# Half-height transposes in the visit of y: 64x128 tiles in pairs, with four PSUM banks

## The chip, the cores and the metric

The kernel runs on one core of a Trainium2 chip. The metric is the device time of one execution, in microseconds. The engines are TensorE (PE, with its weight loads shown apart as PEld), VectorE (DVE), ScalarE (ACT), GpSimd (POOL) and SyncE (SP), which here issues nearly all DMAs.

## The reference

Decayed linear attention over 768 tokens, for 4 batches and 8 heads of 64, and then a feed-forward network with softplus on its 3072 tokens:

```python
gamma = 1.0 - 2.0 ** (-5.0 - np.arange(H))
for t in range(S):
    state = gamma * state + k[t] (outer) v[t]      # per batch and head, 64 x 64
    y[t] = (q[t] @ state) / sqrt(64)
x = y as (3072, 512)
h = x @ w_in                                       # 512 -> 2048
g = np.maximum(h, 0.0) + np.log1p(np.exp(-np.abs(h)))
out = g @ w_out                                    # 2048 -> 512
```

q, k, v are float32; w_in and w_out arrive as 64-bit floats and are converted on the chip.

## The kernel before

**Attention.** It works in 24 chunks of 128 tokens (6 per batch), each for all 8 heads. `unit(m, first, G, when)` makes the operations of chunk m; the first chunk comes in two halves, so there are 25 units, and n counts them from 0. A unit loads q, k and v of the chunk (two, two and one DMA on SP), scales q and v on POOL (L419, L415), and then has three visits to TensorE:

1. *Transposes* (tk and tq, L436): eight of 128x128, four of k and four of q, into two PSUM banks; ACT copies each bank to the tile kt (L443, L444).
2. *Scores* (`scores`): 64 matmuls on 64x64 tiles of the array, four side by side: products of k and q, and the chunk's contribution to the state. DVE masks the products (L463) and adds the state (L472).
3. *y* (`outputs`): 64 matmuls on 64x64 tiles, from the state and the masked products. ACT and DVE add the parts together (L541, L547), and ACT and POOL split the sum into a high and a low part in the tile x (L550, L551).

The pairs of banks of the three visits are called tp, sc and yp. From the sixth unit on all of them are taken out of two banks, a0 and a1 (`ATT`).

**The network.** Blocks of 512 tokens, six of them, each in 16 steps of 128 hidden columns (`ffn_step`). A step has twelve matmuls 128x128 by 512 columns into one of two banks hp0 and hp1 (high and low parts: three products for each of four slices of the model's width). DVE, ACT, DVE, ACT and POOL make softplus and split it into gh and gl (L592 to L596); DVE's L594 is the last that reads hp. Then come twelve matmuls into four banks acc0 to acc3, eight with gh and four with gl. All matmuls but the transposes are issued on one helper line, L328. Weights come in tiles of 512 KB and are converted by ACT, DVE and POOL (L352 to L376); a tile's load waits until the tile `2 * FETCH` places before it has been converted.

**The order.** A planner (`Planner.order`) simulates the engines with costs, hand-over times and due times, and writes out a fixed order for each engine; the engines keep to it. `LEAD`, `STAGE` and `PACE` set due times, `SLOW` scales the costs of ACT, DVE and POOL, `KEEP` weighs changes of the array's tiling, `RESERVE` lets an operation hold back from a shared bank for one that is due sooner. `kind` of a TensorE operation is R128 (dense), T128 (transposes) or Q64 (64x64 tiles).

Of the kernel before, what the change touches and what calls it, by code (L numbers as in the profile page):

```python
# [10 lines left out]
F32 = mybir.dt.float32  # L11
# [5 lines left out]
ALU = mybir.AluOpType  # L17
# [9 lines left out]
ST = 4  # L27
QACT = 1
FENCED = 5
SOON = 1  # L30
ORDER = ('c00', 'c01', 'c1', 'h0', 'c2', 'c3', 'h1')
FETCH = 3
SLACK = 2.0**-17

HANDOVER = {
# [60 lines left out]
class Planner:  # L96
# [5 lines left out]
    def add(self, engine, cost, run, after=(), uses=(), at=None):  # L102
        op = Op(engine, cost, run, after, uses, at)
        op.number = len(self.ops)
        op.both, op.earliest, op.kind = False, 0.0, "R128"
        self.ops.append(op)
        return op

    def order(self):
# [16 lines left out]
        def begin(op, since):  # L126
            taken = {}
            for u in op.uses:
                if u.slot is None:
                    if u.ahead is not None and u.ahead.slot is None:  # L130
                        return 1e12
                    n = taken[u.among[0]] = taken.get(u.among[0], 0) + 1
                    since = max(since, sorted(opens(s, op.engine) for s in u.among)[n - 1])
                if u.among[0] in SHARED:
                    for e, end in u.touched.items():
                        if e != op.engine:
                            since = max(since, end + HANDOVER[e][op.engine])
            return since

        while len(out) < len(self.ops):  # L140
            best, fits, wants = None, {}, []
            for e, cands in ready.items():
                fits[e] = []
                for since, op in cands:
                    b = begin(op, since)
                    if b < 1e12:
                        s = max(free[e], b)
                        fits[e].append((s, b, op))
                        wants += [(op.due, s, op, u) for u in op.uses if u.slot is None and u.among[0] in SHARED]
# [67 lines left out]
RESERVE = 200  # L217
SLOW = 1.02
SHARED = ("hp0", "hp1", "acc0", "acc1", "acc2", "acc3", "a0", "a1")
AHEAD = 1.6  # L220
RAMP = 8
COMFORT = {'PE': 0, 'ACT': 0, 'DVE': 0, 'POOL': 0, 'SP': 0}


@with_exitstack
def decay_attention_then_softplus_ffn(ctx: ExitStack, tc: tile.TileContext, q, k, v, w_in, w_out, qtab, vtab, gtab, out):
# [35 lines left out]
    def buf(held):  # L262
        if held.tile is None:
            held.tile = held.make()
        return held.tile
# [40 lines left out]
    def PE(n, run, after, uses=(), at=None, kind="R128"):  # L306
        op = plan.add("PE", n, run, after, uses, at)
        op.kind = kind
        return op

    def ACT(n, run, after, uses=(), at=None):
        return plan.add("ACT", n, run, after, uses, at)
# [65 lines left out]
            wdone[nm, f] = hi, low_  # L378


    xdone, xread, stlast, states, ys = {}, {}, {}, {}, []

    def unit(m, first, G, when):

        n = len(ys)
        b, c = divmod(m, NC)
        E = 2 * G
        hs = slice(4 * first, 4 * (first + G))
# [45 lines left out]
        def transposes(s, held):  # L434
            for e in range(E):
                emit(nc.tensor.transpose(bank(tp[s])[:, e * C:(e + 1) * C], blocks(held)[:, e], ident))  # L436

        old = lambda by: [ys[n - by]] if n >= by else []
        tk = PE(109 * E, lambda: transposes(0, kn), ldk + old(KT), [tp[0], kn], when[0], "T128")
        tq = PE(109 * E, lambda: transposes(1, qn), [dq] + old(KT), [tp[1], qn], when[0], "T128")  # L440
        turned = lambda s: bank(tp[s])[:, :E * C].rearrange("p (e t) -> p e t", e=E)
        ck = [
            ACT(scalar_time(E * C), lambda: emit(nc.scalar.copy(buf(kt)[:, 0, :E], turned(0))), [tk], [tp[0], kt]),  # L443
            ACT(scalar_time(E * C), lambda: emit(nc.scalar.copy(buf(kt)[:, 1, :E], turned(1))), [tq], [tp[1], kt])  # L444
            if QACT else
            DVE(vector_time(E * C), lambda: emit(nc.vector.tensor_copy(buf(kt)[:, 1, :E], turned(1))), [tq], [tp[1], kt]),
        ]
        part = lambda i: slice(i * D, (i + 1) * D)
        parts = 2 if c < NC - 1 else 1

        def scores():
# [25 lines left out]
        for i_ in range(parts):  # L477
            su.append(DVE(vector_time(E * D), lambda i_=i_: update(i_), [s] + su + (stlast[m - 1] if c else []), [sc[i_], st[i_ + 1]] + [x for x in st[i_:i_ + 1] if x]))
        stlast.setdefault(m, []).append(su[-1])

        if n < FENCED:
            def outputs():
# [27 lines left out]
                        for a in range(2):  # L510
                            inner(1 - r, r, g, a)

            y = PE(E * 117 * (2 if c else 1.5) + 240, outputs, ma + su[:1] + [dv] + ck + (stlast[m - 1] if c else []), yp + [vn, ah, kt] + [x for x in st[:2] if x], when[2], "Q64")
            ys.append(y)
            xdeps = [o for j in range(es.start, es.stop) for o in xread.get((i - 2, j), [])]
            xo = lambda t, r: xt[:, t, off // W, es.start + r:es.stop:2, off % W:off % W + C]
            yo = lambda r: bank(yp[r])[:, :G * C].rearrange("p (g t) -> p g t", g=G)
            xhs = [ACT(scalar_time(G * C), lambda r=r: emit(nc.scalar.copy(xo(0, r), yo(r))), [y] + xdeps, [yp[r]]) for r in range(2)]
            xls = [DVE(vector_time(G * C), lambda r=r: emit(nc.vector.tensor_tensor(xo(1, r), yo(r), xo(0, r).bitcast(F32), op=ALU.subtract)), [xhs[r]] + xdeps, [yp[r]]) for r in range(2)]
            done = list(zip(xhs, xls))  # L520
        else:
            xs = hold_xs()

# [13 lines left out]
            y = PE(E * 117 * (2 if c else 1.5), outputs, ma + su[:1] + [dv] + ck + (stlast[m - 1] if c else []), yp + [vn, ah, kt] + [x for x in st[:2] if x], when[2], "Q64")  # L537
            ys.append(y)
            xdeps = [o for j in range(es.start, es.stop) for o in xread.get((i - 2, j), [])]
            xo = lambda t: xt[:, t, off // W, es, off % W:off % W + C]  # L540
            xa = [ACT(scalar_time(E * D), lambda i=i: emit(nc.scalar.copy(buf(xs)[:, :E, part(i)].rearrange("p (g r) t -> p r g t", r=2), second_half(yp[i]).rearrange("p (r g) t -> p r g t", r=2))), [y], [yp[i], xs]) for i in range(2)]  # L541
            tokens = slice(0, C) if c else part(1)

            def add(r):
                st_ = bank(yp[r])[:, :G * C].rearrange("p (g t) -> p g t", g=G)[:, :, tokens]
                part_ = buf(xs)[:, r:E:2, tokens]
                emit(nc.vector.tensor_tensor(part_, st_, part_, op=ALU.add))  # L547

            xb = [DVE(vector_time(E * D // (1 if c else 2)), lambda r=r: add(r), xa, [yp[r], xs]) for r in range(2)]
            xh = ACT(scalar_time(E * C, False), lambda: emit(nc.scalar.copy(xo(0), buf(xs)[:, :E])), xb + xdeps, [xs])  # L550
            xl = POOL(2.53 * E * C, lambda: emit(nc.gpsimd.tensor_tensor(xo(1), buf(xs)[:, :E], xo(0).bitcast(F32), op=ALU.subtract)), [xh] + xdeps, [xs])  # L551
            done = [(xh, xl)] * 2
        for j in range(es.start, es.stop):
            xdone[m, j] = list(done[j % 2])
# [202 lines left out]
```

## Time and profile before

| what | value |
|---|---|
| times of three runs | 631.61, 633.56, 636.33 us |
| median | 633.56 us |
| the profiled execution's own time | 632.99 us |
| its span, first to last instruction | 631.2 us |
| PE busy | 616.8 us (98%) |
| DVE, ACT, POOL busy | 240.3, 223.6, 239.0 us |
| granted TensorE clock | 1.000 |
| DMA moved | 42.79 MB, mean 68 GB/s |

The page gives busy times, the chain of work that ended last (followed back from the last instruction, at each step to what released it), groups of instructions by line and shape, and DMA issues. The timeline's rows have start and length in microseconds, the engine, the line, the operation, what it writes and reads, and how many instructions are merged in the row; a bracket holds the idle time before it and who ended it. Matmuls are pipelined: a record of 0.39 us does not keep the array for 0.39 us. The price of a matmul is the distance to the next one's start.

### The profile page before, as it was taken

How to read it: one execution, taken by the hardware profiler on the slowest of the kernel's cores; microseconds unless marked ns; L12 is line 12 of the kernel's file. 1: busy time of each engine (PE TensorE's matmuls, PEld its weight loads, DVE VectorE, ACT ScalarE, POOL GpSimd, SP SyncE). 2: the span in 40 equal slices, each digit the busy share in tenths (PEclk: the TensorE clock that was granted, in tenths of full speed). 3: DMA queues.
4: the chain of work that ended last, by engine and by line, in shares of the span. 5: the costliest groups of instructions: out<-in, count | busy, mean ns of one | idle time of the engine just before them, and what ended most of it. 6: DMA issues, size and time to landing. Idle time of an engine off the chain costs nothing.

```text
span 631.2 us, 12857 instructions
## 1 busy us (share of the span) xinstructions
PE 616.8 (98%) x5464; PEld 505.8 (80%) x5464; DVE 240.3 (38%) x439; ACT 223.6 (35%) x405; POOL 239.0 (38%) x206
## 2 busy tenths in 40 slices
PE   5889999999999999999999999999999999999997
PEld 4778888778888888888888888888888888888886
DVE  3687789343333223323333223233332322322232
ACT  3577877333223223222233222322332223322221
POOL 3577777553333324233333242333323223212221
PEclk9999999999999999999999999999999999999999
DMA  7997661341211203102113021020320000100001
GB/s 190 276 297 243 199 208 61 69 128 25 51 27 26 51 9 110 34 18 51 24 28 107 18 46 34 18 51 22 97 52 0 2 1 1 67 1 2 0 1 66
DMA packets 90441, 42.79 MB, mean 68 GB/s; under 512 B 77072, under 2 KB 85264, under 8 KB 90384
## 3 DMA queue, kind: packets, MB, share of 16 engines
q1 hardware_dynamic: 89936, 41.95, 24.1%
q8 instruction: 43, 0.70, 0.4%
q14 instruction: 14, 0.11, 0.1%
q10 hardware_dynamic: 448, 0.01, 0.0%
HBM read 35.66 MB, written 6.29 MB: 66 GB/s over the span
## 4 chain that ended last, share of the span: by engine, by line
PE 97%; DMA 1%; ACT 1%; DVE 1%; issue 1%; SPq 0%; POOL 0%; DVEq 0%; ACTq 0%; POOLq 0%
PE acc L328 43%; PE hp L328 43%; PE a L328 7%; PE a L436 3%; DMA qn<-in_q_dram 1%; PE acc L436 0%; DVE ah L463 0%; ACT win L375 0%; DVE a L367 0%; DVE a L362 0%; DVE st L472 0%; POOL qn L419 0%; ACT wout L375 0%; ACT wout L444 0%; ACT w L631 0%
## 5 line engine op out<-in xcount | busy, mean ns | idle before, releaser
L328 PE MATMUL hp<-x,win 128*128 128x512 f32 (+1 forms) x1176 | 289.2, 390 | 0.0
L328 PEld LDWEIGHTS hp<-x,win 128*128 128x128 f32 x1176 | 215.3, 189 | 43.2
L596 POOL TENSOR_TENSOR gl<-sp,gh 128x512 fp32r<-128x512 f32 x90 | 115.9, 1288 | 320.8 <-ACT gh L595 218.9
L328 PE MATMUL acc<-wout,gh 128*128 128x512 f32 x736 | 190.3, 394 | 0.0
L328 PEld LDWEIGHTS acc<-wout,gh 128*128 128x128 f32 x736 | 136.3, 188 | 29.7
L592 DVE TENSOR_SCALAR sp<-hp 128x512 uint32<-128x512 uint32 x92 | 63.5, 690 | 239.2 <-PE hp L328 188.1
L593 ACT ACTIVATE sp<-sp 128x512 f32<-128x512 f32 x92 | 58.1, 632 | 228.2 <-DVE sp L592 228.1
L328 PE MATMUL acc<-wout,gl 128*128 128x512 f32 x368 | 103.0, 390 | 0.0
L594 DVE SCALAR_TENSOR_TENSOR sp<-hp,sp 128x512 f32<-128x512 f32 x92 | 63.5, 690 | 55.6 <-ACT sp L593 55.5
L328 PEld LDWEIGHTS acc<-wout,gl 128*128 128x128 f32 x368 | 69.0, 188 | 14.7 <-POOL gl L596 0.2
L595 ACT CAST gh<-sp 128x512 fp32r<-128x512 f32 x90 | 55.9, 621 | 43.8 <-DVE sp L594 43.0
L443 ACT COPY kt<-a 128x512 f32<-128x512 f32 (+1 forms) x22 | 12.7, 576 | 63.5 <-PE a L436 63.4
L463 DVE TENSOR_TENSOR ah<-a,mask 128x256 uint32<-128x256 uint32 x42 | 15.9, 419 | 36.2 <-PE a L328 36.2
L551 POOL TENSOR_TENSOR x<-xs,x 128x512 fp32r<-128x512 f32 x20 | 25.8, 1289 | 8.9 <-ACT x L550 8.9
L419 POOL TENSOR_TENSOR qn<-qn,tabs 128x512 f32<-128x512 f32 (+1 forms) x23 | 23.8, 1033 | 8.8 <-DMA qn<-in_q_dram 8.6
L415 POOL TENSOR_TENSOR vn<-vn,tabs 128x512 f32<-128x512 f32 (+1 forms) x24 | 24.2, 1008 | 5.7 <-DMA vn<-in_v_dram 5.7
L376 POOL TENSOR_TENSOR wout<-w,wout 128x512 fp32r<-128x512 f32 x16 | 20.7, 1294 | 8.6 <-ACT wout L375 8.6
L376 POOL TENSOR_TENSOR win<-w,win 128x512 fp32r<-128x512 f32 x16 | 20.7, 1297 | 8.0 <-ACT win L375 5.2
L352 ACT ACTIVATE raw<-raw 128x512 f32<-128x512 f32 x32 | 21.2, 677 | 2.4 <-DMA raw<-in_moe_w_in_dram 2.3
L367 DVE SCALAR_TENSOR_TENSOR a<-raw,a 128x512 uint32<-128x512 uint32 x28 | 19.1, 690 | 1.4 <-ACT a L356 1.0
L547 DVE TENSOR_TENSOR xs<-a,xs 128x256 f32<-128x256 f32 (+1 forms) x40 | 14.3, 395 | 12.6 <-ACT xs L541 12.6
L372 DVE SCALAR_TENSOR_TENSOR w<-raw,a 128x512 uint32<-128x512 uint32 x28 | 18.6, 679 | 0.6
(106 smaller groups left out, 377.4 us busy)
## 6 DMA issues: line engine op xcount, KB each, us to landing
raw<-in_moe_w_in_dram SPq DMA_DIRECT2D x16, 512.0 KB, 6.8
raw<-in_moe_w_out_dram SPq DMA_DIRECT2D x16, 512.0 KB, 5.9
qn<-in_q_dram SPq DMA_DIRECT2D x44, 128.0 KB, 2.6
kn<-in_k_dram SPq DMA_DIRECT2D x44, 128.0 KB, 2.8
vn<-in_v_dram SPq DMA_DIRECT2D x22, 256.0 KB, 3.0
out_dram<-w SPq DMA_DIRECT2D x22, 256.0 KB, 2.2
out_dram<-win SPq DMA_DIRECT2D x2, 256.0 KB, 2.1
qn<-in_q_dram SPq DMA_DIRECT2D x4, 64.0 KB, 2.3
```

What stands on the lines that cost most here:

```text
L328: mm = lambda o, l, r, start, stop: emit(nc.tensor.matmul(o, lhsT=l, rhs=r, start=start, stop=stop))
L352: a = ACT(685, lambda word=word: emit(nc.scalar.activation(word(1).bitcast(F32), word(1).bitcast(F32), AF.Copy, scale=2.0**-112)), [ld], [ ...
L367: lambda word=word, wp=wp: emit(nc.vector.scalar_tensor_tensor(bits(wp), word(1), 0x80000000, bits(wp), op0=ALU.bitwise_and, op1=ALU.bitwi ...
L376: low_ = POOL(1300, lambda nm=nm, w=w: emit(nc.gpsimd.tensor_tensor(hl(nm, f)[:, 1], buf(w), hl(nm, f)[:, 0].bitcast(F32), op=ALU.subtract ...
L415: emit(engine.tensor_tensor(heads(held), heads(held), by, op=ALU.mult))
L419: emit(engine.tensor_tensor(all_, all_, by, op=ALU.mult))
L551: xl = POOL(2.53 * E * C, lambda: emit(nc.gpsimd.tensor_tensor(xo(1), buf(xs)[:, :E], xo(0).bitcast(F32), op=ALU.subtract)), [xh] + xdeps, ...
L592: a = DVE(vector_time(T), lambda: emit(nc.vector.tensor_scalar(U(spv()), U(bank(hp)), 0x80000000, None, op0=ALU.bitwise_or)), [lasts[-1]] ...
L593: b = ACT(640, lambda: emit(nc.scalar.activation(spv(), spv(), AF.Softplus)), [a], [sp])
L594: c = DVE(vector_time(T), lambda: emit(nc.vector.scalar_tensor_tensor(spv(), bank(hp), 0.0, spv(), op0=ALU.max, op1=ALU.add)), [b], [hp, sp])
L595: e = ACT(scalar_time(T, False), lambda: emit(nc.scalar.copy(buf(gh), spv())), [c], [sp, gh])
L596: g = POOL(1300, lambda: emit(nc.gpsimd.tensor_tensor(buf(gl), spv(), buf(gh).bitcast(F32), op=ALU.subtract)), [e], [sp, gh, gl])
```

## The change

From the 13th unit on (`MERGED = 12`) the transposes of a unit are no visit of their own. They are sixteen transposes of 64 rows by 128 columns, two for each of the eight blocks, one on the upper and one on the lower half of the rows. Those of the lower half of the tokens go to one bank, those of the upper half to the other, for k and q together; the copies to kt write the halves of the tokens accordingly. They are issued in one operation of the planner together with the y of the unit before (`outputs_and_turn`), whose planning is held back in the list `pending` until the next unit comes. This operation needs four banks, and banks of the attention are now taken out of a0, a1, hp0 and hp1 (`WIDE`). It is "patient": another operation that wants one of its banks holds back when the patient one could start within `HOLD`, 1000 ns. Numbers of the planner change with it (`FETCH`, `KEEP`, `LEAD`, `PACE`, `SLOW`, `COMFORT`).

```diff
+MERGED = 12
+HOLD = 1000
-FETCH = 3
+FETCH = 2
...
                     b = begin(op, since)
+                    if op.patient:
+                        wants += [(op.due, max(free[e], since), op, u) for u in op.uses if u.slot is None and u.among[0] in SHARED]
...
-                        rivals = sum(d < op.due and t < s + RESERVE and o is not op and set(v.among) <= set(u.among) for d, t, o, v in wants)
+                        rivals = sum(d < op.due and t < s + (HOLD if o.patient else RESERVE) and o is not op and not set(v.among).isdisjoint(u.among) for d, t, o, v in wants)
...
-KEEP = 2
+KEEP = 0.5
-LEAD = 2700
+LEAD = -4000
-PACE = 500
+PACE = 0
-SLOW = 1.02
+SLOW = 1.0
+WIDE = ["a0", "a1", "hp0", "hp1"]
-COMFORT = {'PE': 0, 'ACT': 0, 'DVE': 0, 'POOL': 0, 'SP': 0}
+COMFORT = {'PE': 0, 'ACT': 100, 'DVE': 100, 'POOL': 100, 'SP': 0}
...
-        banks = [[hold_bank(ATT[0]) for _ in range(2)] for _ in range(3)]
-        tp, sc, yp = banks
+        merged = n >= MERGED
+        tp = [hold_bank(WIDE if merged else ATT[0]) for _ in range(2)]
+        sc = [hold_bank(WIDE if n >= MERGED else ATT[0]) for _ in range(2)]
+        yp = [hold_bank(WIDE if n + 1 >= MERGED else ATT[0]) for _ in range(2)]
...
+        if merged:
+            def turn():
+                for t, held in enumerate((kn, qn)):
+                    for e in range(E):
+                        for i in range(2):
+                            emit(nc.tensor.transpose(bank(tp[i])[:, (t * E + e) * D:(t * E + e + 1) * D], blocks(held)[side[i], e], ident[side[i], part(i)]))
+
+            tdeps, tuses = ldk + [dq] + old(KT), [*tp, kn, qn]
+            if pending:
+                outputs_, cost_, deps_, uses_, _, finish_ = pending.pop()[1:]
+
+                def outputs_and_turn():
+                    outputs_()
+                    turn()
+
+                tk = tq = PE(cost_ + 58 * 2 * E, outputs_and_turn, deps_ + tdeps, uses_ + tuses, when[0], "Q64")
+                tk.patient = True
+                finish_(tk)
+            else:
+                tk = tq = PE(58 * 2 * E, turn, tdeps, tuses, when[0], "Q64")
+            turned = lambda i: bank(tp[i])[:, :2 * E * D].rearrange("p (s e t) -> p s e t", s=2, e=E)
+            into = lambda i: buf(kt)[:, :, :E, part(i)]
+        else:
...
         ck = [
-            ACT(scalar_time(E * C), lambda: emit(nc.scalar.copy(buf(kt)[:, 0, :E], turned(0))), [tk], [tp[0], kt]),
-            ACT(scalar_time(E * C), lambda: emit(nc.scalar.copy(buf(kt)[:, 1, :E], turned(1))), [tq], [tp[1], kt])
+            ACT(scalar_time(E * C), lambda: emit(nc.scalar.copy(into(0), turned(0))), [tk], [tp[0], kt]),
+            ACT(scalar_time(E * C), lambda: emit(nc.scalar.copy(into(1), turned(1))), [tq], [tp[1], kt])
...
+        deps = ma + su[:1] + [dv] + ck + (stlast[m - 1] if c else [])
+        uses = yp + [vn, ah, kt] + [x for x in st[:2] if x]
+        pending.append((m, outputs, cost, deps, uses, when[2], finish))
+        if n + 1 < MERGED:
+            flush()
+
+    def flush():
+        if pending:
+            m, outputs, cost, deps, uses, due, finish = pending.pop()
+            finish(PE(cost, outputs, deps, uses, due, "Q64"))
...
     def ffn_step(s, h, i, f, when):
+        if pending and pending[0][0] < NT * (i + 1):
+            flush()
```

More of the change, by code (lines that the diff above doesn't have):

```diff
@@ L104, in add @@
         op.number = len(self.ops)
-        op.both, op.earliest, op.kind = False, 0.0, "R128"
+        op.both, op.earliest, op.kind, op.patient = False, 0.0, "R128", False
         self.ops.append(op)
@@ L148, in order @@
                         fits[e].append((s, b, op))
-                        wants += [(op.due, s, op, u) for u in op.uses if u.slot is None and u.among[0] in SHARED]
+                        if not op.patient:
+                            wants += [(op.due, s, op, u) for u in op.uses if u.slot is None and u.among[0] in SHARED]
             def waits(s, op):
@@ L378, in convert_weights @@
             wdone[nm, f] = hi, low_
-    xdone, xread, stlast, states, ys = {}, {}, {}, {}, []
+    xdone, xread, stlast, states, ys, pending = {}, {}, {}, {}, [], []
     def unit(m, first, G, when):
-        n = len(ys)
+        n = len(ys) + len(pending)
         b, c = divmod(m, NC)
@@ L432, in unit @@
         xt = X[i % 2]
-        def transposes(s, held):
-            for e in range(E):
-                emit(nc.tensor.transpose(bank(tp[s])[:, e * C:(e + 1) * C], blocks(held)[:, e], ident))
         old = lambda by: [ys[n - by]] if n >= by else []
-        tk = PE(109 * E, lambda: transposes(0, kn), ldk + old(KT), [tp[0], kn], when[0], "T128")
-        tq = PE(109 * E, lambda: transposes(1, qn), [dq] + old(KT), [tp[1], qn], when[0], "T128")
-        turned = lambda s: bank(tp[s])[:, :E * C].rearrange("p (e t) -> p e t", e=E)
+        part = lambda i: slice(i * D, (i + 1) * D)
@@ new lines, in unit, with transposes @@
+        if merged:
[18 more added lines that the diff above has]
+        else:
+            def transposes(s, held):
+                for e in range(E):
+                    emit(nc.tensor.transpose(bank(tp[s])[:, e * C:(e + 1) * C], blocks(held)[:, e], ident))
+            tk = PE(109 * E, lambda: transposes(0, kn), ldk + old(KT), [tp[0], kn], when[0], "T128")
+            tq = PE(109 * E, lambda: transposes(1, qn), [dq] + old(KT), [tp[1], qn], when[0], "T128")
+            turned = lambda s: bank(tp[s])[:, :E * C].rearrange("p (e t) -> p e t", e=E)
+            into = lambda s: buf(kt)[:, s, :E]
@@ L442, in unit @@
         ck = [
-            ACT(scalar_time(E * C), lambda: emit(nc.scalar.copy(buf(kt)[:, 0, :E], turned(0))), [tk], [tp[0], kt]),
-            ACT(scalar_time(E * C), lambda: emit(nc.scalar.copy(buf(kt)[:, 1, :E], turned(1))), [tq], [tp[1], kt])
+            ACT(scalar_time(E * C), lambda: emit(nc.scalar.copy(into(0), turned(0))), [tk], [tp[0], kt]),
+            ACT(scalar_time(E * C), lambda: emit(nc.scalar.copy(into(1), turned(1))), [tq], [tp[1], kt])
             if QACT else
-            DVE(vector_time(E * C), lambda: emit(nc.vector.tensor_copy(buf(kt)[:, 1, :E], turned(1))), [tq], [tp[1], kt]),
+            DVE(vector_time(E * C), lambda: emit(nc.vector.tensor_copy(into(1), turned(1))), [tq], [tp[1], kt]),
@@ L447, in unit @@
         ]
-        part = lambda i: slice(i * D, (i + 1) * D)
         parts = 2 if c < NC - 1 else 1
@@ L479, in unit, with record @@
         stlast.setdefault(m, []).append(su[-1])
+        def record(done):
+            for j in range(es.start, es.stop):
+                xdone[m, j] = list(done[j % 2])
         if n < FENCED:
@@ L511, in outputs, with finish @@
                             inner(1 - r, r, g, a)
[L513 to L520, printed above, removed]
+            cost = E * 117 * (2 if c else 1.5) + 240
+            def finish(y):
+                ys.append(y)
+                xdeps = [o for j in range(es.start, es.stop) for o in xread.get((i - 2, j), [])]
+                xo = lambda t, r: xt[:, t, off // W, es.start + r:es.stop:2, off % W:off % W + C]
+                yo = lambda r: bank(yp[r])[:, :G * C].rearrange("p (g t) -> p g t", g=G)
+                xhs = [ACT(scalar_time(G * C), lambda r=r: emit(nc.scalar.copy(xo(0, r), yo(r))), [y] + xdeps, [yp[r]]) for r in range(2)]
+                xls = [DVE(vector_time(G * C), lambda r=r: emit(nc.vector.tensor_tensor(xo(1, r), yo(r), xo(0, r).bitcast(F32), op=ALU.subtract)), [xhs[r]] + xdeps, [yp[r]]) for r in range(2)]
+                record(list(zip(xhs, xls)))
         else:
@@ L535, in outputs @@
                                 mm(second_half(yp[i])[side[a], r * G + g], heads(vn)[side[i], 4 * g + 2 * r + a], buf(ah)[side[i], r, a * G + g], True, True)
[L537 to L554, printed above, removed]
+            cost = E * 117 * (2 if c else 1.5)
@@ new lines, in finish, with add @@
+            def finish(y):
+                ys.append(y)
+                xdeps = [o for j in range(es.start, es.stop) for o in xread.get((i - 2, j), [])]
+                xo = lambda t: xt[:, t, off // W, es, off % W:off % W + C]
+                xa = [ACT(scalar_time(E * D), lambda i=i: emit(nc.scalar.copy(buf(xs)[:, :E, part(i)].rearrange("p (g r) t -> p r g t", r=2), second_half(yp[i]).rearrange("p (r g) t -> p r g t", r=2))), [y], [yp[i], xs]) for i in range(2)]
+                tokens = slice(0, C) if c else part(1)
+                def add(r):
+                    st_ = bank(yp[r])[:, :G * C].rearrange("p (g t) -> p g t", g=G)[:, :, tokens]
+                    part_ = buf(xs)[:, r:E:2, tokens]
+                    emit(nc.vector.tensor_tensor(part_, st_, part_, op=ALU.add))
+                xb = [DVE(vector_time(E * D // (1 if c else 2)), lambda r=r: add(r), xa, [yp[r], xs]) for r in range(2)]
+                xh = ACT(scalar_time(E * C, False), lambda: emit(nc.scalar.copy(xo(0), buf(xs)[:, :E])), xb + xdeps, [xs])
+                xl = POOL(2.53 * E * C, lambda: emit(nc.gpsimd.tensor_tensor(xo(1), buf(xs)[:, :E], xo(0).bitcast(F32), op=ALU.subtract)), [xh] + xdeps, [xs])
+                record([(xh, xl)] * 2)
```

## The prediction

> **What bounds the kernel now.** I read the page's busy times and its chain first, then the sums by stretch, then TensorE's waits, then the timeline of one chunk.
>
> ```profile
> span 631.2 us, 12857 instructions
> PE 616.8 (98%) x5464; PEld 505.8 (80%) x5464; DVE 240.3 (38%) x439; ACT 223.6 (35%) x405; POOL 239.0 (38%) x206
> PE 97%; DMA 1%; ACT 1%; DVE 1%; issue 1%; SPq 0%; POOL 0%; DVEq 0%; ACTq 0%; POOLq 0%
> ```
> ```profile
> 0.00:47.00 47.00, 36.35 (x614) 31.02 (x615) 28.19 (x66) 24.78 (x50) 24.32 (x31) 1.00 0.94 254
> 47.00:142.00 95.00, 94.98 (x987) 77.15 (x986) 65.07 (x115) 60.44 (x110) 64.31 (x53) 1.00 0.50 152
> 142.00:521.00 379.00, 379.00 (x3399) 309.94 (x3397) 116.83 (x213) 110.01 (x201) 123.28 (x102) 1.00 0.15 38
> 521.00:631.20 110.20, 106.50 (x476) 87.64 (x468) 30.20 (x45) 28.39 (x47) 27.08 (x21) 1.00 0.05 20
> ```
> ```profile
> PE a L436 <- DVE qn L419: 4.3, 1, 4.3
> PE a L328 <- DVE st L472: 1.5, 1, 1.5
> ```
>
> The columns of the second fence are the stretch, its length, then busy time of PE, weight loads, DVE, ACT and POOL, the granted clock, the DMA share and GB/s. TensorE owns 97% of the chain. From 47 us on it never stands still: 94.98 of 95 us, then 379.00 of 379. The 10.65 us that it idles lie in the first 47 us, where DMA is at 0.94; the largest TensorE wait is the very first, for q. So behind 47 us a change can only win by giving TensorE less to do, and can lose wherever TensorE has to wait. A busy record says little of the price of one instruction, because the records overlap; prices must come from starts. Here is one chunk, with the other engines' rows that matter later.
>
> ```profile
> 298.08 4.24 PE L328 MATMUL hp<-x,win 128*128 128x512 f32 x18
> 302.16 1.98 PE L328 MATMUL acc<-wout,gh 128*128 128x512 f32 x8
> ...
> 306.24 2.00 PE L328 MATMUL acc<-wout,gh 128*128 128x512 f32 x8
> 308.08 1.07 PE L328 MATMUL acc<-wout,gl 128*128 128x512 f32 x4
> 308.99 0.85 PE L328 MATMUL hp<-x,win 128*128 128x512 f32 x3
> 309.68 0.60 PE L436 MATMUL a<-ident,kn 128*128 128x128 f32 x4
> 309.94 0.69 DVE L592 TENSOR_SCALAR sp<-hp 128x512 uint32<-128x512 uint32 x1 [4.63 <-PE hp L328]
> 310.11 0.60 PE L436 MATMUL a<-ident,qn 128*128 128x128 f32 x4
> 310.31 0.59 ACT L443 COPY kt<-a 128x512 f32<-128x512 f32 x1 [4.29 <-PE a L436]
> 310.46 2.30 PE L328 MATMUL hp<-x,win 128*128 128x512 f32 x9
> 310.79 0.64 ACT L593 ACTIVATE sp<-sp 128x512 f32<-128x512 f32 x1
> 311.46 0.69 DVE L594 SCALAR_TENSOR_TENSOR sp<-hp,sp 128x512 f32<-128x512 f32 x1 [0.82 <-ACT sp L593]
> 312.69 0.69 PE L328 MATMUL a<-kt 64*64 64x64 f32 x32
> 313.21 0.65 PE L328 MATMUL a<-vn,kn 64*64 64x64 f32 x32
> 313.79 2.11 PE L328 MATMUL acc<-wout,gh 128*128 128x512 f32 x8
> 315.74 1.07 PE L328 MATMUL acc<-wout,gl 128*128 128x512 f32 x4
> 316.64 0.84 PE L328 MATMUL hp<-x,win 128*128 128x512 f32 x3
> 317.41 0.69 PE L328 MATMUL a<-kt,st 64*64 64x64 f32 x32
> 317.93 0.65 PE L328 MATMUL a<-ah,vn 64*64 64x64 f32 x32
> 318.51 2.34 PE L328 MATMUL hp<-x,win 128*128 128x512 f32 x9
> 318.85 0.63 ACT L541 COPY xs<-a 128x256 f32<-128x256 f32 x2
> 319.59 0.74 DVE L547 TENSOR_TENSOR xs<-a,xs 128x256 f32<-128x256 f32 x2
> 320.68 1.98 PE L328 MATMUL acc<-wout,gh 128*128 128x512 f32 x8
> ```
> ```profile
> L328 PE MATMUL a<-ah,vn 64*64 64x64 f32 x480 | 9.7, 218 | 0.0
> L436 PE MATMUL a<-ident,qn 128*128 128x128 f32 x60 | 9.0, 272 | 0.0
> ```
>
> The visits of a chunk are the transposes (309.68), the scores (312.69) and y (317.41). A dense matmul costs (302.16 − 298.08)/18 = 0.227 us. Whatever a dense run takes beyond that is the price of going in or out of a visit.
>
> **The change part by part.**
>
> *The transposes go.* Their eight starts last 310.46 − 309.68 = 0.78 us. The nine dense matmuls behind them take 2.23 us against 9 × 0.227 = 2.04, so 0.19 too much; 0.09 of it belongs to entering the scores, since the three dense ones ahead of y also take 0.77 instead of 0.68. Leaving the transposes costs 0.10. Removed: 0.88 us per chunk. One transpose costs (0.60 − 0.272)/3 = 0.109 us.
>
> *Sixteen half tiles come.* Each has 64 rows, 128 columns and 64 moving columns, and they stand in pairs, one on either half of the rows. No row of before has this form. The ends: a pair runs at the pace of a set of four 64x64 matmuls, at most (0.65 − 0.218)/7 = 0.06 us, so 8 × 0.06 = 0.48; or a pair costs what a transpose of 128 columns costs, 8 × 0.109 = 0.87; or the two of a pair don't run beside each other, 16 × 0.109 = 1.74. I take 0.06. The reason is in the lengths of the records:
>
> ```profile
> L328 PE MATMUL hp<-x,win 128*128 128x512 f32 x10 | 2.5, 392 | 0.0
> L328 PE MATMUL hp<-x,win 128*128 128x256 f32 x17 | 2.2, 283 | 0.0
> ```
>
> A transpose with 128 moving columns (272 ns) is as long as a dense matmul with 256 (283 ns) and far from the one with 512. A 64x64 one is 54 ns shorter. So both kinds behave as if the moving side set the pace, at some 0.43 ns (109/256) for each of two steps per column, and the moving side is what this change halves. The ends of records are modelled, so this is a leaning and no proof.
>
> The Trainium skill speaks against it: "TensorE: Matmul & The Clock Gate", section "LDWEIGHTS (loading the stationary operand)", says that a load's time follows the stationary columns alone, whatever the rows, at 107 ns for 128. The trace fits that as well (109 ns per transpose, 60 per set with 64 columns), since in every form of before the two sides are equally wide. By that page a pair would cost as much as a whole transpose and the first term of the sum below would be nothing.
>
> *The change of tile inside the visit.* Between y's 64x64 tiles and the 64x128 tiles the array's division changes. Ends: nothing, and the 0.09 + 0.13 = 0.22 us that going in and out of a y visit costs (0.13 is 318.51 to 320.68, 2.17, less 2.04). Half the division, the rows, stays; I take 0.11. The skill's "TensorEngine Tiling (Array Packing)", section "Key Properties", says that every change of mode drains the engine; by it I would take the upper end. Leaving the visit costs what leaving y costs already.
>
> *Sum on TensorE:* 0.88 − 0.48 − 0.11 = 0.29 us for each fused visit. Unit 12's transposes ride on unit 11's y, and so on up to unit 24: 13 visits, 13 × 0.29 = 3.8 us.
>
> *Four banks for a visit.* It needs both y banks and both transpose banks, out of a0, a1, hp0, hp1: all four at once. Before, y needed two and a half-filled hp stayed beside it (316.64 and 318.51). Now TensorE's queue, which is in order, holds the acc and hp matmuls behind a visit that waits for DVE's last read of hp (L594), for DVE's reads of the scores (L463, L472), for POOL's scaled q of the next chunk (L419) and for its k. From TensorE's turning away (309.68) to the end of that L594 (311.46 + 0.69) are 2.47 us. The twelve acc matmuls of the step before are 12 × 0.227 = 2.72, so they cover it with 0.25 to spare, if they all stand there. After the visit the banks come free through two copies of 0.59, two L541 (0.63) and two L547 (0.74): at most 2.55 us one after another, again under 2.72. POOL waits for ACT's gh in this order as before. I take nothing; the upper end is under the rivals. An end below nothing is excluded behind 47 us, since no wait is there to win.
>
> *Moved work.* Copies, masks, y's parts and loads stay the same in number; the two copies write runs of 64, as L541's do at their usual pace. ACT, DVE and POOL are busy under a third of 142 to 521 us, which hides them. Due times of units come 6.7 us earlier (LEAD), those of steps no longer drift (PACE); loads of q, k and v move up on SP past output stores, with DMA at 0.15 there. POOL's scaling moves up past gl; it takes 123 of 379 us. If that cover were gone, a visit would wait for one such operation, about 1 us.
>
> *The start.* FETCH 2 lets four weight tiles be on their way in place of six, and the other planner numbers (KEEP, SLOW, COMFORT, HOLD) may reorder it.
>
> ```profile
> raw<-in_moe_w_in_dram SPq DMA_DIRECT2D x16, 512.0 KB, 6.8
> L367 DVE SCALAR_TENSOR_TENSOR a<-raw,a 128x512 uint32<-128x512 uint32 x28 | 19.1, 690 | 1.4 <-ACT a L356 1.0
> ```
>
> A tile takes 6.8 us to land and five operations of about 0.69, some 10.3 us; four at a time make two tiles in 5.2 us. A step wants two tiles in 24 × 0.227 us plus a quarter of a chunk's visits (a quarter of 3.5), 6.3 us. So the loads stay hidden with 1.1 us a step to spare; without that cover, DVE being busy 65 of 95 us there, each of the 14 later steps could lose a few tenths, 4 us in all. On the other side at most the 10.65 idle us of the start can be won. I take nothing.
>
> The profiled execution took 632.99 us with its span of 631.2; its time lies 0.57 below the median of the runs, 633.56. 632.99 − 3.8 = **629.2 us**.
>
> **The rivals.**
>
> *The pair is held by its 128 columns.* 0.88 − 0.87 − 0.11 = −0.10, times 13: 634.3 us. For it: the equal widths above cannot exclude it. Against it: the record lengths. This is the skill's rule on the load, above.
>
> *Four banks make TensorE wait* (the one that ends slower). Place: ahead of each fused visit. If only the eight gh matmuls are there as cover (1.82 us), 2.47 − 1.82 = 0.65 us is open: 13 × 0.65 = 8.5, less 3.8, gives 637.7 us. With only four gl matmuls it is 1.56 us a visit and 649. It decides from 0.29 us a visit on. For it: hp is never free in the rows above, one half-filled group always lies across a visit. Against it: the planner orders with nearly these durations, and its order of before leaves TensorE no wait behind 47 us.
>
> *The start gets shorter as well*, by a third of its idle time, 3.5 us: 625.7 us. For it: fewer weight tiles ahead of q, k, v at a DMA share of 0.94. Against it: TensorE's first weights, which bound the first dense run, are no earlier.
>
> *The tiles don't run two at a time* (the change does not do what it says): at 0.109 each, 0.88 − 1.74 − 0.11 = −0.97, 645.6 us; at 0.06 each 635.6. Against it: four 64x64 tiles do run together in before.
>
> **How the numbers follow.** Forecast 0.49, column-bound pair 0.22, bank waits 0.14, shorter start 0.10, no pairs 0.05. The range reaches from 625.0 (just past the shorter start) to 637.7 (the first bank-wait case); outside lie the longer bank waits, unpaired tiles at 0.109 and a start shortened further. A measurement of this kernel tells about 1%, 6.3 us, from no change. Faster by over that, below 627.2: the shorter start (0.10), plus the part of the forecast without a price for the change of tile (627.8) and with any gain at the start, 0.12: 0.22. Slower by over it, above 639.9: longer bank waits 0.06, no pairs 0.03, late weights 0.02: 0.11. Within: 0.67.
>
> **What would show it.** Starts of a fused visit's pairs 0.06 apart (right) or 0.11 (rival); the time from y's last start to the first transpose for the change of tile; a chunk from visit to visit in about 25.0 us in place of 25.3; TensorE waits for hp's L594 for the banks; idle TensorE time up to 47 us for the start. The prediction is wrong if pairs cost 0.11 or any wait of TensorE's behind 47 us sums to over 4 us.

## The result and the profile after

The changed kernel takes 629.62 us (median of 6 runs, 628.59 to 631.87) against 633.74 us (6 runs, 631.61 to 636.33) for the kernel before beside it: a ratio of 0.9932 with the interval 0.9906 to 0.9957. The forecast was 629.2. The profiled execution took 629.27 us. First the page of the changed kernel (its span, its busy times, its chain by engine), then its sums by stretch, with the columns of the prediction's second fence:

```profile
span 627.6 us, 13098 instructions
PE 612.6 (98%) x5568; PEld 501.7 (80%) x5568; DVE 242.7 (39%) x439; ACT 225.3 (36%) x405; POOL 239.3 (38%) x206
PE 93%; DMA 2%; issue 1%; POOL 1%; SPq 1%; DVE 1%; ACT 0%; POOLq 0%; DVEq 0%
```
```profile
0.00:47.00 47.00, 37.51 (x685) 31.77 (x686) 29.82 (x71) 25.32 (x50) 26.97 (x33) 1.00 0.92 244
47.00:142.00 95.00, 93.89 (x922) 76.11 (x921) 64.37 (x114) 61.87 (x113) 64.76 (x53) 1.00 0.52 155
142.00:521.00 379.00, 378.36 (x3513) 308.95 (x3512) 119.49 (x214) 112.09 (x202) 122.99 (x102) 1.00 0.15 38
521.00:627.60 106.60, 102.81 (x454) 84.83 (x452) 28.97 (x42) 26.06 (x42) 24.62 (x20) 0.99 0.06 20
```

TensorE is still the bound. There are 104 more matmul records (13 chunks, eight more transposes each), and yet less busy time. What is new is idle time behind 47 us, where before TensorE hardly ever stood still: 1.11 us in the second row, ahead of the fused visits (0.70 for POOL's gl at 59.35, and 0.41 at 93.68 for which the trace names no releaser), and 0.64 us in the third.

One fused visit in the timeline of the changed kernel; L334 is the helper that was L328, L449 the half transposes:

```profile
276.00 0.69 PE L334 MATMUL a<-kt,st 64*64 64x64 f32 x32
276.51 0.65 PE L334 MATMUL a<-ah,vn 64*64 64x64 f32 x32
277.09 0.46 PE L449 MATMUL hp<-ident,kn 64*128 64x64 f32 x8
277.38 0.42 PE L449 MATMUL hp<-ident,qn 64*128 64x64 f32 x8
277.73 1.20 PE L334 MATMUL acc<-wout,gh 128*128 128x512 f32 x4
...
301.05 0.69 PE L334 MATMUL a<-kt,st 64*64 64x64 f32 x32
```
```profile
L449 PE MATMUL hp<-ident,kn 64*128 64x64 f32 x104 | 6.7, 236 | 0.6 <-DVE sp L645 0.4
L449 PE MATMUL hp<-ident,qn 64*128 64x64 f32 x104 | 5.5, 223 | 0.0
```

From the first transpose to the first dense matmul are 277.73 − 277.09 = 0.64 us. The row of q has eight transposes in four pairs and is 0.42 long with one record of 0.223, so its pairs start (0.42 − 0.223)/3 = 0.066 us apart; in the unmerged starts it is 0.0626. Eight pairs make 0.50, and 0.14 is left for the change of tile. A chunk, from one y to the next, takes 301.05 − 276.00 = 25.05 us; before, it was 309.68 − 284.36 = 25.32.

**How the gain divides.** A simple measure: the time from the start of the 11th unit's y to the last dense matmul, less 0.2269 us for each dense matmul started in between. What is left is what the attention's visits and the waits cost. Before (two rows), then after:

```profile
165.68 0.69 PE L328 MATMUL a<-kt,st 64*64 64x64 f32 x32
...
627.12 0.39 PE L328 MATMUL acc<-wout,gl 128*128 128x512 f32 x1
```
```profile
158.79 0.69 PE L334 MATMUL a<-kt,st 64*64 64x64 f32 x32
...
623.42 0.39 PE L334 MATMUL acc<-wout,gl 128*128 128x512 f32 x1
```

Between them stand 1812 dense matmuls before and 1836 after (24 of them moved behind that y). Before: 627.12 − 165.68 − 1812 × 0.2269 = 50.30 us. After: 623.42 − 158.79 − 1836 × 0.2269 = 48.05 us. So 2.25 us are won there, not 3.8. The two executions are 3.72 us apart; the other 1.4 us lie ahead of that point (158.79 + 24 × 0.2269 = 164.24 against 165.68).

**Where the visits lose.** Three of the 13 fused visits wait, at 251.40, 352.31 and 452.79, some 100 us or one block of the network apart. The first one, with the other engines' rows:

```profile
249.54 1.07 PE L334 MATMUL acc<-wout,gl 128*128 128x512 f32 x4
...
250.54 0.46 PE L334 MATMUL a<-kt,st 64*64 64x64 f32 x16
...
250.82 0.65 PE L334 MATMUL a<-ah,vn 64*64 64x64 f32 x32
251.20 0.69 DVE L645 SCALAR_TENSOR_TENSOR sp<-hp,sp 128x512 f32<-128x512 f32 x1 [0.70 <-ACT sp L644]
...
251.40 0.27 PE L449 MATMUL hp<-ident,kn 64*128 64x64 f32 x1
...
252.04 0.43 PE L449 MATMUL hp<-ident,kn 64*128 64x64 f32 x7 [0.37 <-DVE sp L645]
252.28 0.44 PE L449 MATMUL hp<-ident,qn 64*128 64x64 f32 x8
...
252.66 0.73 PE L334 MATMUL acc<-wout,gh 128*128 128x512 f32 x2
```

The first transpose goes to the one hp bank, which is free; the second goes to the other, whose last reader L645 (L594 before) ends at 251.89. TensorE turned away from that bank at 249.54, so the chain of softplus took 2.35 us to that end (the prediction has 2.47), and the next transpose starts 2.50 us after the turning away. In that time TensorE had only four matmuls with gl and a y shortened to 48 matmuls (the first chunk of a batch has no state): 251.40 − 249.54 = 1.86 us. The visit is 1.26 us in place of 0.64. At the other two y is whole and the visits last 1.02. The three cost 0.61 + 0.38 + 0.38 = 1.37 us. With 13 × 0.27 = 3.5 for the chunks, 3.5 − 1.4 = 2.1 stands against the 2.25 measured. In the ten other visits hp was read out long before.

### The profile page after: what moved, and what is told of

Same layout as the page of the kernel before. It is cut to its first block, busy times and chain, and to the rows that moved or that the text cites. A ratio compares the mean times of both kernels' runs of the same rounds, so it can differ in the third digit from the quotient of the medians.

```text
span 627.6 us, 13098 instructions
## 1 busy us (share of the span) xinstructions
PE 612.6 (98%) x5568; PEld 501.7 (80%) x5568; DVE 242.7 (39%) x439; ACT 225.3 (36%) x405; POOL 239.3 (38%) x206
## 4 chain that ended last, share of the span: by engine, by line
PE 93%; DMA 2%; issue 1%; POOL 1%; SPq 1%; DVE 1%; ACT 0%; POOLq 0%; DVEq 0%
PE hp L334 43%; PE acc L334 42%; PE a L334 5%; DMA qn<-in_q_dram 2%; PE hp L449 1%; PE a L469 1%; POOL win L382 0%; SPq L412 0%; POOL qn L425 0%; DVE sp L643 0%; DVE sp L645 0%; SPq L353 0%; ACT sp L644 0%; POOL gl L647 0%; POOL vn L421 0%
## 5 line engine op out<-in xcount | busy, mean ns | idle before, releaser
L334 PE MATMUL hp<-x,win 128*128 128x512 f32 (+1 forms) x1176 | 296.1, 388 | 0.0
L334 PEld LDWEIGHTS hp<-x,win 128*128 128x128 f32 x1176 | 215.5, 188 | 44.0
L334 PE MATMUL acc<-wout,gh 128*128 128x512 f32 x736 | 197.9, 393 | 0.0
L334 PEld LDWEIGHTS acc<-wout,gh 128*128 128x128 f32 x736 | 136.3, 188 | 29.3 <-ACT gh L646 0.2
L644 ACT ACTIVATE sp<-sp 128x512 f32<-128x512 f32 x92 | 58.1, 632 | 247.8 <-DVE sp L643 247.7
L334 PE MATMUL acc<-wout,gl 128*128 128x512 f32 x368 | 103.1, 391 | 0.7 <-POOL gl L647 0.7
L645 DVE SCALAR_TENSOR_TENSOR sp<-hp,sp 128x512 f32<-128x512 f32 x92 | 63.5, 691 | 53.5 <-ACT sp L644 53.1
L334 PEld LDWEIGHTS acc<-wout,gl 128*128 128x128 f32 x368 | 68.9, 188 | 15.6 <-POOL gl L647 1.1
L590 ACT CAST x<-xs 128x512 fp32r<-128x512 f32 x20 | 12.4, 619 | 15.0 <-DVE xs L587 15.0
L334 PEld LDWEIGHTS a<-kt,st 64*64 64x64 f32 x616 | 11.4, 135 | 7.6 <-issue 6.9
```

The costliest lines, as they stand in the source:

```text
L334: mm = lambda o, l, r, start, stop: emit(nc.tensor.matmul(o, lhsT=l, rhs=r, start=start, stop=stop))
L644: b = ACT(640, lambda: emit(nc.scalar.activation(spv(), spv(), AF.Softplus)), [a], [sp])
L645: c = DVE(vector_time(T), lambda: emit(nc.vector.scalar_tensor_tensor(spv(), bank(hp), 0.0, spv(), op0=ALU.max, op1=ALU.add)), [b], [hp, sp])
```

## The experiments

The kernels with other transposes, with plain matmuls, with the half tiles apart and with `HOLD = 0` were timed in a single run each, which can't tell 2 us from nothing on this kernel; they are read from their timelines. The first three and the half tiles apart had one run of the kernel before beside them, of 631.52 us.

**Whole transposes in the fused visit.**

```diff
-                        for i in range(2):
-                            emit(nc.tensor.transpose(bank(tp[i])[...], blocks(held)[side[i], e], ident[side[i], part(i)]))
+                        emit(nc.tensor.transpose(bank(tp[t])[:, e * C:(e + 1) * C], blocks(held)[:, e], ident))
```

> The fused visits keep their place and order, but the transposes in them are eight of 128x128 again, k into one bank and q into the other. Theory (the gain comes from pairs at 0.062 us): first transpose to first dense matmul 8 x 0.109 + 0.145 for the change of tile = 1.02 us in place of 0.645; a chunk 25.4 us in place of 25.05; 13 x 0.37 = 4.9 us more, 634 us. Rival (the gain comes from having one visit less and from the new order): 0.65 to 0.7 us, a chunk near 25.05, 629 to 630 us.

634.39 us. The fused visit in its timeline:

```profile
229.31 0.65 PE L448 MATMUL hp<-ident,kn 128*128 128x128 f32 x4
229.80 0.60 PE L448 MATMUL hp<-ident,qn 128*128 128x128 f32 x4
230.16 1.17 PE L334 MATMUL acc<-wout,gh 128*128 128x512 f32 x4
```

230.16 − 229.31 = 0.85 us, 0.2 more than the half tiles; a chunk is 25.24 us, and the measure above gives 50.57, that is 2.5 us more than after. Of these, 2.1 are ten visits at 0.21 (the three visits that wait for hp last as long as after, 1.25 and 1.02 us), and 0.5 is one wait for DVE's copy out of an acc bank (L683). So the half tiles are worth having, at about half the expected price a visit: among dense matmuls the same eight transposes took 0.78 us, so the change of tile cost the whole ones 0.07, where 0.145 on top of 8 × 0.109 had been expected.

**The same sixteen transposes, all of the upper half's after all of the lower's.**

```diff
-                for t, held in enumerate((kn, qn)):
-                    for e in range(E):
-                        for i in range(2):
+                for i in range(2):
+                    for t, held in enumerate((kn, qn)):
+                        for e in range(E):
```

> The same sixteen 64x128 transposes, but first the eight of the lower rows and then the eight of the upper rows, so that neighbours use the same half of the array. Theory (a pair is two tiles side by side, each held by its 64 moving columns): 16 x 0.062 + 0.145 = 1.14 us in place of 0.645, 13 x 0.5 = 6.4 us more, 635.7 us. Rival A (a tile is held by its 128 loaded columns and only the other half of the rows hid that): 16 x 0.109 + 0.145 = 1.89 us, 16 us more, 645.5 us. Rival B (half a tile has half the price, neighbours do not matter): 0.645 us, 629.3 us.

634.26 us. In its timeline:

```profile
228.90 0.46 PE L449 MATMUL hp<-ident,kn 64*128 64x64 f32 x4
229.19 0.22 PE L449 MATMUL hp<-ident,qn 64*128 64x64 f32 x1
229.20 0.27 PE L449 MATMUL hp<-ident,kn 64*128 64x64 f32 x1
...
229.50 0.41 PE L449 MATMUL hp<-ident,qn 64*128 64x64 f32 x4
229.84 1.20 PE L334 MATMUL acc<-wout,gh 128*128 128x512 f32 x4
```

The visit takes 229.84 − 228.90 = 0.94 us in place of 0.64. As long as only lower tiles run, single ones start 0.0626 us apart, exactly as pairs do in the changed kernel: two at a time cost what one costs. It isn't the whole 0.50 more, because k's upper tiles (from 229.20) start while q's lower ones are still being started. That tiles run in pairs is shown.

**Sixteen plain matmuls with half the moving columns, in the place of the transposes.**

```diff
-emit(nc.tensor.transpose(bank(tp[i])[...], blocks(held)[side[i], e], ident[side[i], part(i)]))
+mm(bank(tp[i])[...], blocks(held)[:, e], ident[:, part(i)], True, True)
```

> The same sixteen results from tiles of all 128 rows: 128 columns loaded, 64 moving (half of the identity), as plain matmuls, since such a tile cannot have a neighbour beside it. This measures what sets the pace of one instruction. Theory (the moving columns): 0.06 us from start to start, 16 x 0.06 + 0.1 = 1.1 us in place of 0.645, 635 us. Rival (the 128 loaded columns): 0.109 each, 1.85 us, 645 us.

667.54 us. In its timeline:

```profile
228.39 2.00 PE L334 MATMUL hp<-ident,kn 128*128 128x64 f32 x16
230.22 1.95 PE L334 MATMUL hp<-ident,qn 128*128 128x64 f32 x16
231.98 1.18 PE L334 MATMUL acc<-wout,gh 128*128 128x512 f32 x4
```

3.59 us, which neither theory had: 32 records for 16 matmuls, 3.59/32 = 0.112 us each. A plain float32 matmul is two records here and a transpose is one (the 64 matmuls of a scores or a y visit, counted by their records, are 32 in the program), so this test changed more than the moving side. It says nothing of transposes by itself; but at 64 moving columns a record still took what 128 loaded columns take.

**The pairs as plain matmuls**, run later to repair that test: the same tiles of 64 rows, loaded columns and moving columns as in the changed kernel, only not as transposes.

```diff
+mm(bank(tp[i])[...], blocks(held)[side[i], e], ident[side[i], part(i)], True, True)
```

> The sixteen half tiles again in pairs of 64x128, 128 columns loaded and 64 moving, but as plain matmuls with the identity; with tiles of all 128 rows such matmuls were two records of 0.111 us each. It tells whether half the rows or the transpose itself makes the half tile cheap. Theory (half the rows are what makes it cheap, whatever the instruction): 32 records a visit in 16 pairs of 0.06 us, 16 x 0.0625 + 0.15 = 1.15 us in place of 0.645. Rival (128 loaded columns cost 0.11 in a plain matmul for any number of rows, and only the transpose escapes that): 16 x 0.111 + 0.15 = 1.93 us.

647.58 us. In its timeline:

```profile
227.80 1.11 PE L334 MATMUL hp<-ident,kn 64*128 64x64 f32 x16
228.74 1.06 PE L334 MATMUL hp<-ident,qn 64*128 64x64 f32 x16
229.73 1.20 PE L334 MATMUL acc<-wout,gh 128*128 128x512 f32 x4
```

229.73 − 227.80 = 1.93 us: 16 pairs of records, again 0.11 apart. For plain matmuls the loaded columns set the pace, with 64 rows as with 128. Only the transpose runs at 0.0626 with 128 loaded and 64 moving columns.

**Half tiles in a visit of their own.**

```diff
-            if pending:
+            if False:
...
-        if n + 1 < MERGED:
-            flush()
+        flush()
```

> The half tiles stay, but they are a visit of their own, from the 13th unit on, with two banks; y is a visit of its own as before. Theory (fusing matters because going in and out costs 0.09 + 0.22 us and 64x128 tiles pay that while 128x128 ones pay 0.10): 0.50 + 0.05 + 0.31 = 0.86 us for the transposes against 0.88 before the change, a chunk 25.3 us, and no waits for banks: 13 x 0.26 more and 1.1 less than the changed kernel, about 631.5 us. Rival (the tiles alone bring the gain): a chunk near 25.05 us and 628 to 629 us.

634.79 us. In its timeline:

```profile
230.39 0.46 PE L449 MATMUL a<-ident,kn 64*128 64x64 f32 x8
230.68 0.42 PE L449 MATMUL a<-ident,qn 64*128 64x64 f32 x8
231.03 1.65 PE L334 MATMUL hp<-x,win 128*128 128x512 f32 x6
```

The transposes last 0.64 us here too, but a chunk takes 25.28 us (255.43 to 280.71), as the theory had it: next to no gain. What the narrow tiles save on themselves is lost in going from dense matmuls to them and out again. What the theory had wrong is the banks: TensorE waits four times for the last read of hp (L644 here), 1.4 us in all, and the measure gives 51.00 us, 1.45 more than the planner's numbers alone (the next kernel).

**The planner's numbers alone**; the transposes stay whole and apart.

```diff
-MERGED = 12
+MERGED = 99
```

> All of the planner's new numbers, no fused visit at all (MERGED = 99), so every unit has its 128x128 transposes in two banks. Theory (the numbers gain 1.4 us in the first 180 us, and nothing after it): TensorE reaches the transposes of the 12th unit as early as in the changed kernel, chunks take 25.3 us from there, about 632 us. Rival (the numbers gain nothing, the early gain belongs to the fused units): about 633.5 us.

632.42 us (630.88 to 633.24, 10 runs) against 633.69 (35 runs), a ratio of 0.9977 with 0.9957 to 0.9997. From one chunk's transposes to the next, in its timeline:

```profile
279.74 0.60 PE L469 MATMUL a<-ident,kn 128*128 128x128 f32 x4
...
305.03 0.60 PE L469 MATMUL a<-ident,kn 128*128 128x128 f32 x4
```

25.29 us. By the measure it leaves 49.55 us: of the 2.25 us won, the numbers bring 0.75 by themselves. With the three others this makes a table of a chunk's length: before 25.32, numbers only 25.29, whole transposes in the visit 25.24, half tiles in their own visit 25.28, both together 25.05. Either half of the change is worth under 0.1 us by itself; together they save 0.24 over the numbers.

The start was compared here as well. Up to the 12th unit this kernel's order is that of the changed kernel, yet it came there 2.5 us later. The first run of dense matmuls with one weight tile, before, after and in this kernel:

```profile
25.32 4.08 PE L328 MATMUL hp<-x,win 128*128 128x256 f32 x24
```
```profile
24.36 3.14 PE L334 MATMUL hp<-x,win 128*128 128x256 f32 x24
```
```profile
25.12 4.25 PE L334 MATMUL hp<-x,win 128*128 128x256 f32 x24
```

In the profiled execution of the changed kernel these 24 matmuls were 0.94 us shorter than before. Their distance is 0.21 us up to some point and 0.12 from there on, and that point differs from run to run: the granted clock is full from 27.5 us on before, from 21.9 after, and in other kernels with the same order up to there from some point between 20.5 and 37.9 us on (the latest one, late banks below, was at full from 27.7 and back at half from 34.5 to 37.9). The clock isn't all of it. The half tiles in a visit of their own had it full from 22.1 us and took 3.14 us for these 24 matmuls too, but came to the 11th unit's y at 161.37, 2.6 us later than the changed kernel: TensorE stood idle for 2.08 us before 33.35, and the trace names no releaser. Late banks has such a gap of 1.42 us, the changed kernel none there. So the 1.4 us ahead of the 11th unit's y can't be credited to the change.

**FETCH back to 3** in the changed kernel.

```diff
-FETCH = 2
+FETCH = 3
```

> The changed kernel with six weight tiles on their way (FETCH = 3) as before. Theory (four tiles in place of six let q, k and v of the first chunks land sooner): the early gain of 1.4 us goes, 631 us. Rival (the early gain comes from other numbers, FETCH does nothing): 629.6 us.

630.11 us (10 runs), a ratio of 0.9946 (0.9927 to 0.9965): no loss that shows. The smaller reach of the loads does nothing that shows, in either direction.

**The transposes' banks counted as needed later.** The planner asks for all four banks at a fused visit's start, though the transposes come after y.

```diff
-since = max(since, sorted(opens(s, op.engine) for s in u.among)[n - 1])
+since = max(since, sorted(opens(s, op.engine) for s in u.among)[n - 1] - op.late.get(u, 0))
...
+                tk.late = dict.fromkeys(tp, cost_)
```

> The planner is told that the two transpose banks of a fused visit are first written behind y's matmuls, by the planner's own cost for y later than the visit's start; nothing else changes. Theory (the three waits of 0.38 us for hp come from an order made with all four banks counted as needed at once): the order moves fused visits earlier, the three waits shrink or go, 0.5 to 1.1 us less, 628.5 to 629.1 us. Rival (that early order only moves the wait from the plan to the chip): waits at more visits than three, 630 us or more.

631.54 us (628.5 to 633.1, 12 runs), a ratio of 0.9963 (0.994 to 0.9986). The theory fell: every engine's order came out as in the changed kernel, with two banks exchanged, and the three waits are there. So this is a second measurement of the same order. The mean of its 12 runs and the 6 of the changed kernel is 630.7 us, about 3 us below the kernel before.

**The same, fused from the 11th unit on.**

```diff
-MERGED = 12
+MERGED = 10
```

> As the kernel with late banks, and fused from the 11th unit on: two fused visits more. Theory (each fused visit gains 0.28 us if nothing waits): 0.5 us less than late banks, 628 to 628.6 us. Rival (in the block where weights are still converted the four banks are missed): equal or slower than late banks.

631.87 us (12 runs), 0.9974 (0.9954 to 0.9993): no gain over the one above. There are two more fused visits, and one more of them waits (four now); TensorE also waits 0.7 us once for DVE's copy out of an acc bank (L685), which the kernel above doesn't.

**Nothing holds back for a fused visit.**

```diff
-HOLD = 1000
+HOLD = 0
```

> The changed kernel with HOLD = 0: no other operation holds back from a0, a1, hp0 or hp1 for the sake of a fused visit. Theory (the holding back keeps the four banks from costing TensorE time; without it a fused visit finds hp filled again and the order gets later visits and stretches without work): TensorE idles at most fused visits and around them, 10 us or more above the changed kernel, over 640 us. Rival (four banks are no constraint worth speaking of): 629 to 632 us, waits of 0.38 us at three visits at most.

660.25 us, at a granted clock of 0.98 in the stretch below. Its sums by stretch, the largest of TensorE's waits, and from its timeline a y and the two visits behind it:

```profile
200.00:550.00 350.00, 335.96 (x2865) 275.07 (x2865) 101.65 (x178) 95.06 (x169) 104.62 (x86) 0.98 0.14 35
```
```profile
PE hp L334 <- ACT kt L476: 6.4, 9, 1.0
```
```profile
236.24 0.69 PE L334 MATMUL a<-kt,st 64*64 64x64 f32 x32
...
238.72 0.33 PE L334 MATMUL hp<-kt 64*64 64x64 f32 x2 [0.67 <-ACT kt L476]
...
241.63 0.70 PE L334 MATMUL a<-kt,st 64*64 64x64 f32 x16 [1.27 <-DVE st L506]
```

14 us idle in 350, about half of the 30 us by which this kernel is slower; the clock stood at half for two times 6.8 us of the stretch, and the rest wasn't divided up. Visits come in bunches: y with its transposes, scores, and the next y, each waiting for the copies (L476) or the states (L506) of the one before, with no dense work between. That a fused visit is put off until four banks are free, and the next ones then fall together, is how I read it; one such delay wasn't followed back. The rival of the four banks is a real mechanism; the rule that others hold back is what keeps it small.

**Late banks, fused from the 11th unit on, and the steps due earlier** by 200 ns more at each.

```diff
-MERGED = 12
+MERGED = 10
...
-PACE = 0
+PACE = -200
```

> Late banks, fused from the 11th unit on, and PACE = -200, so that the steps' due times come closer together and fused visits are ordered relative to them in another way. Theory (the three waits come from fused visits that have only four gl matmuls and y between the last hp group and the transposes; another order gives them more): no wait at any fused visit, from the 12th unit's scores on 1.1 us less than the changed kernel, 0.5 us more from two further fused visits, 629 us against 630.7 (the mean of the changed kernel and of late banks, whose order is the same). Rival (the waits move elsewhere): 630.5 us or more.

628.66 us (626.67 to 631.34, 6 runs) against 633.50 (11 runs), a ratio of 0.9926 (0.9897 to 0.9955). The visit that waited in the changed kernel:

```profile
249.54 0.69 DVE L646 SCALAR_TENSOR_TENSOR sp<-hp,sp 128x512 f32<-128x512 f32 x1 [0.70 <-ACT sp L645]
...
250.69 0.46 PE L334 MATMUL a<-kt,st 64*64 64x64 f32 x16
...
251.55 0.46 PE L449 MATMUL hp<-ident,kn 64*128 64x64 f32 x8
...
252.19 1.20 PE L334 MATMUL acc<-wout,gh 128*128 128x512 f32 x4
```

The last read of hp now ends at 250.23, ahead of the visit, and the transposes take 0.64 us. No fused visit waits, and the measure gives 46.24 us, 1.8 less than after: 1.4 of it the waits, some 0.25 the one further fused visit that lies in this stretch (the other lies ahead of it); 0.2 us are left over.

**The same, fused from the 9th unit on.**

```diff
-MERGED = 10
+MERGED = 8
```

> As the kernel before it, but fused from the 9th unit on, while weights are still being converted. Theory (a fused visit gains 0.28 us there too): 0.5 us less, about 628.5 us. Rival (the conversions' use of ACT, DVE and of a0 and a1 makes fused visits wait): 630 us or more.

627.99 us (626.78 to 629.1, 6 runs), a ratio of 0.9912 (0.9891 to 0.9932). This is the best version. It beats the kernel before clearly, and its interval lies wholly below that of the second measurement of the changed order (0.994 to 0.9986); against the first (0.9906 to 0.9957) they overlap, so the step from the changed kernel is 1.6 us by the one median and 3.6 by the other, and not measured closer.

## Why the prediction was right, and where it wasn't

*The pair.* "I take 0.06" was right, at 0.0626, and with it the first and largest term, 0.50 for 0.48. The rival of the 128 columns (0.109) is out for the transposes, and so is that of tiles not running two at a time. The reason given, that "both kinds behave as if the moving side set the pace", can hold only for one kind. Plain matmuls with 64 rows, 128 loaded and 64 moving columns took 0.11 us a record, so the 64x64 matmuls, with the same rows and moving columns, owed their 0.06 to their 64 loaded columns, and the forecast got the transposes right by a reading of record lengths that was false for the others. The Trainium skill, "TensorE: Matmul & The Clock Gate", section "LDWEIGHTS (loading the stationary operand)", puts 128 columns at 107 ns whatever the rows: the two plain runs agree (0.11 with 128 rows and with 64), the transposes of the changed kernel do not (0.0626 for the same 128 columns). The same page's section "Terms" speaks of a transpose mode that is four times faster for float32; a plain pair costs two records, 0.22 us, against 0.0626, a factor of 3.5 here. That "in every form of before the two sides are equally wide" passes over the dense matmuls, but those with 256 moving and 128 loaded columns, 0.12 us apart at full clock, fit either side. The records of the loads show a difference as well, in the pairs as plain matmuls and in the changed kernel:

```profile
L334 PEld LDWEIGHTS hp<-ident,kn 64*128 64x128 f32 x192 | 12.5, 187 | 1.3 <-issue 0.3
```
```profile
L449 PEld LDWEIGHTS hp<-ident,kn 64*128 64x128 f32 x104 | 4.6, 137 | 1.8 <-PE a L334 1.0
```

The load of a half transpose is 137 ns long where the same load of a plain matmul is 187; whole transposes have 139, and plain loads of 64 columns 135. That makes it likely that the load isn't what sets a transpose's pace. Why it is shorter stays open, and so does whether the half rows or the half moving columns make the half transpose cheap, since a transpose halves both together.

*The change of tile.* 0.11 was taken between 0 and 0.22; it is 0.14. With the pair, a visit won 0.27 instead of 0.29. That is well placed, though 0.03 of it comes from the planner's numbers, which were costed at nothing.

*The four banks.* "I take nothing" failed, by 1.37 us. The chain of 2.47 us was right; the cover was "the twelve acc matmuls of the step before (…) if they all stand there", and at three visits only four stood there. What the prediction didn't see is that y itself is cover, since its own banks are a0 and a1 and only the transposes touch hp. So a visit with four acc matmuls pays 0.38 or 0.61, not the 1.56 us of the rival. The rival's place and price per lost matmul were right, its count (13 visits) wasn't: 3.

*The sum.* 3.8 us were expected behind the first fused visit; 2.25 came. Of the 4.1 us between the medians, then, nearly half isn't in any term of the sum.

*The start.* "I take nothing" stands, as far as these runs tell: the profiled execution came through the start 1.4 us earlier, but executions of one order differ there by up to 4.7. In this pair 0.94 us of it are the 24 matmuls that ran at full clock sooner. That the total hit within 0.5 us is this luck and the bank waits cancelling each other. Over all 18 runs of that order the gain is about 3 us, and 630.7 would have been the right number.

## What to carry to other kernels

When a small visit to another tile size costs as much in going in and out as in work, join it to a visit that is already there and narrow its tiles together: one of the two alone won under 0.1 us a chunk here, both won 0.24. An operation that needs several buffers waits for each only at its first use, so order it with its early part as cover, and look for the few places where the long chain in front of it has lost that cover. Compare kernels of this size over a stretch with a counted load (time less matmuls times their pace) before crediting a change with what the start of one run did.

## What was not expected of the hardware

- A transpose of float32 with 64 rows, 128 loaded and 64 moving columns starts every 0.0626 us, and two on different halves of the rows together cost the same; a plain matmul of that form takes two records of 0.11 us.
- Transposes on the upper rows started beside ones on the lower rows that stand ahead of them in the program: in the run with the rows in turn, k's upper tiles from 229.20 us, q's last lower ones at 229.38.
- The moment from which TensorE's granted clock stays full varied between 20.5 and 37.9 us among executions with the same order up to there, and the 11th unit's y came between 163.2 and 167.9 us (counted with equal dense work). On 630 us that is as much as the whole change. The clock explains it in part only, since two executions with the full clock from 21.9 and 22.1 us lie 2.6 us apart at that y. Why both vary wasn't found.
